# Fused local/global attention and Mish MLP on one core: sums of squares on ScalarE, clears on VectorE, and a new order for the first stretch

## The chip, the cores and the metric

The kernel runs on one core of one Trainium2 chip. The metric is the device time of one execution in microseconds (us). Lower is better. TensorE (PE) does the matmuls, VectorE (DVE), ScalarE (ACT) and GpSimd (POOL) the rest of the arithmetic; SyncE (SP), ACT and POOL also issue DMA transfers, each into a queue of its own.

## What is computed

The reference, cut to what matters (8 batches, 8 heads, 512 local and 32 global rows, head size 64):

```python
s_g = scale * np.matmul(q_g, k_all.transpose(0, 1, 3, 2))
out_g = np.matmul(sm(s_g), v_all)
...
mask = np.abs(pos[:, None] - pos[None, :]) <= window
s_ll = np.where(mask, s_ll, -1000000000.0)
...
a_l = sm(s_l)
out_l = np.matmul(a_l, np.concatenate([v_g, v_l], axis=2))
...
h = x @ w_in
sp = np.where(h > 20.0, h, np.log1p(np.exp(np.minimum(h, 20.0))))
g = h * np.tanh(sp)
return (g @ w_out).astype(np.float32)
```

Attention of 512 local rows (a window of 32 and the 32 global columns) and of 32 global rows, then a two-layer MLP of width 2048 over all 4352 rows. The two weight matrices come as 64-bit floats.

## The kernel before, in words

**Precision.** Large products are made of fp16 pieces: each operand is scaled by a power of two and split into a high and a low half (three matmuls in place of one). So each tensor needs a scale before it can be split: for a weight matrix from the sum of squares of its entries (bf16 matmuls, `ws`, line 646, and `w_norm`), for a batch's values V from their largest magnitude: `b_max` (line 717) runs five `tensor_reduce` on DVE (lines 729 and 733) into the columns of `vmx`, takes their maximum (line 735), POOL reduces it over the partitions (line 740), and `b_scale` makes the scale `sv` from it. The scale need not be the largest magnitude; anything that bounds the values within the range of fp16 does.

**Weights.** Each matrix is loaded in 16 pieces of 512 KB of raw 64-bit words (`w_load`, lines 598 and 601; the first five issued by ACT, the rest by POOL). DVE turns the words into 32-bit floats in three instructions a piece (`w_bits` line 616, `w_sum` lines 623 and 625). The raw words of the first 16 pieces use seven places in turn, so piece k + 7 can only be loaded when DVE has finished piece k. Then come the norm, the scale `sw`, and the splits (lines 694 to 700).

**The first stretch.** The program begins with loads (`ORDER` and the loop behind it): `qk` tiles of 704 KB (one per head pair of batch 0: queries and keys), `consts` of 272 KB (the mask and an identity matrix), `vraw` of 1024 KB and `vgraw` of 64 KB (batch 0's values), and the weights. For each head pair and tile of 128 rows PE makes scores `s` (line 880), DVE adds the mask and takes the row's extreme in one instruction (`row_max`, line 906, which reads `consts`), ACT takes the exponential (line 915), the probabilities are turned (in batch 0's first half by PE, lines 956 and 970) and multiplied by V (`U`, line 1005), DVE normalizes (`x`, line 1015), PE turns `x` (`XT`, lines 981 and 989), and from the x of all four head pairs the MLP's first matmuls run (`h`, line 1158). In names such as `s_1_0`, the last head pair and half come in this order.

**What sets the order.** Tasks are given to a planner (`Plan`), which lays them on the engines by costs; `moved` then applies a table `MOVES`: "91 P 271" takes task 91 out of its lane and puts it on PE's lane behind task 271 (-1: at the front). Each engine then executes its lane strictly in that order. `kept` (line 428) makes tiles that have to be cleared once: three `P`, two `ph`, four `vc`, four `vgg`, one `gph`, by memsets on POOL. A `partition_all_reduce` on a tile `warm` (line 1862) runs once on POOL ahead of the others. DMA issues of SP and ACT use eight semaphores in turn; an issue waits until the transfer that used its semaphore last has landed.

Of the kernel before, what the change touches and what calls it, by code (L numbers as in the profile page):

```python
# [71 lines left out]

MOVES = [(int(n), e, int(m)) for n, e, m in (x.split() for x in """91 P 271, 92 P 91, 93 P 92, 307 P 95, 284 P 275, 154 P 313, 350 P 154, 318 P 159, 164 P 330, 169 P 422, 174 P 343, 175 P 348, 358 P 356, 176 P 358, 447 P 376, 177 P 378, 178 P 392,
389 P 397, 415 P 461, 179 P 421, 180 P 453, 454 P 180, 181 P 454, 450 P 474, 182 P 450, 183 P 510, 184 P 183, 468 P 184, 533 P 185, 532 P 516, 513 P 556, 565 P 526, 573 P 565, 580
P 562, 625 P 629, 35 V 18, 36 V 19, 37 V 20, 38 V 22, 232 V 39, 233 V 46, 43 V 233, 47 V 43, 44 V 47, 261 V 50, 262 V 54, 58 V 262, 56 V 62, 282 V 67, 283 V 71, 291 V 283, 296 V
291, 76 V 296, 267 V 81, 72 V 267, 73 V 83, 78 V 87, 292 V 88, 115 V 292, 111 V 115, 112 V 268, 274 V 297, 107 V 327, 101 V 107, 108 V 309, 103 V 322, 298 V 103, 104 V 298, 113 V
104, 116 V 380, 328 V 116, 352 V 329, 127 V 366, 131 V 127, 373 V 424, 129 V 133, 374 V 129, 381 V 136, 407 V 139, 137 V 407, 387 V 137, 403 V 387, 388 V 144, 370 V 388, 151 V 370,
371 V 151, 413 V 371, 372 V 413, 414 V 372, 418 V 414, 408 V 418, 384 V 408, 385 V 145, 148 V 448, 383 V 153, 431 V 156, 412 V 161, 419 V 158, 449 V 419, 471 V 449, 149 V 471, 420
V 149, 466 V 420, 396 V 466, 434 V 166, 446 V 459, 163 V 171, 168 V 172, 173 V 168, 429 V 173, 472 V 429, 186 V 529, 511 V 480, 473 V 511, 534 V 188, 483 V 189, 457 V 483, 191 V
410, 478 V 522, 512 V 478, 540 V 524, 535 V 540, 489 V 535, 444 V 195, 906 V 444, 530 V 906, 500 V 530, 220 V 536, 907 V 220, 550 V 571, 552 V 260, 520 V 560, 583 V 520, 584 V 583,  # L80
587 V 585, 590 V 587, 280 V 649, 569 V 280, 639 V 569, 620 V 639, 961 V 960, 554 V 961, 786 V 554, 962 V 610, 1001 V 643, 644 V 1001, 575 V 1003, 687 V 1004, 657 V 1005, 621 V
1035, 1208 V 658, 678 V 1036, 667 V 678, 1037 V 631, 1209 V 632, 637 V 683, 1039 V 724, 813 V 1039, 779 V 734, 761 V 790, 744 V 816, 1127 V 744, 1146 V 1127, 826 V 817, 1147 V 826,
787 V 823, 834 V 787, 797 V 834, 1148 V 797, 798 V 876, 802 V 798, 837 V 802, 235 A 226, 294 A 286, 295 A 294, 105 A 304, 317 A 105, 316 A 314, 312 A 316, 325 A 312, 326 A 335, 355
A 340, 342 A 438, 345 A 342, 440 A 344, 402 A 440, 349 A 357, 359 A 349, 364 A 362, 416 A 377, 417 A 382, 451 A 417, 430 A 451, 395 A 445, 433 A 395, 427 A 458, 452 A 427, 469 A
452, 479 A 469, 428 A 479, 456 A 476, 190 A 482, 192 A 443, 538 A 192, 539 A 538, 514 A 194, 544 A 527, 229 A 548, 528 A 229, 570 A 528, 549 A 570, 519 A 259, 551 A 519, 909 A 563,
567 A 582, 568 A 567, 646 A 626, 656 A 627""".split(","))]
# [1857 lines left out]
```

## Time and profile before

| | before |
|---|---|
| median of 3 runs | 875.17 us (873.54 to 877.06) |
| the profiled execution: its own time | 874.79 us |
| its span in the trace | 873.0 us |
| PE busy | 841.1 us (96%) |
| DVE busy | 747.4 us (86%) |
| ACT busy | 645.9 us (74%) |
| POOL busy | 169.8 us (19%) |
| DMA moved | 111.07 MB |

Busy time is the time in which an engine executes instructions; DMA issues and waits are not in it. The profiled execution took 1.8 us longer than its span, and 0.4 us less than the median of the runs. All stretches below are in microseconds from the span's start.

### The profile page before, as it was taken

What the parts mean: (1) busy time and instruction counts of PE and PEld (TensorE: products, weight loads), DVE (VectorE), ACT (ScalarE), POOL (GpSimd) and SP (SyncE); (2) the same over time, 40 slices, a digit from 0 to 9 for tenths busy, and PEclk for the clock granted to TensorE, in tenths of its full rate; (3) what the DMA queues carried; (4) which work ended last, traced back from release to release, by engine and by line L of the source; (5) the groups of instructions that cost most, each with busy time, mean ns of one, the idle gap of its engine ahead of it and who ended that gap; (6) DMA issues with size and microseconds to landing.
All of it is one profiled execution on the core that took longest, in us unless ns stands there. A gap on an engine that the chain in (4) does not pass through costs nothing.

```text
span 873.0 us, 24744 instructions
## 1 busy us (share of the span) xinstructions
PE 841.1 (96%) x9792; PEld 621.1 (71%) x9792; DVE 747.4 (86%) x1989; ACT 645.9 (74%) x1389; POOL 169.8 (19%) x324
## 2 busy tenths in 40 slices
PE   2789999999999999999999999999999999999997
...
DVE  6998999758897799999879986998789999986675
...
DMA  9978566365998976769566785475757641000000
GB/s 366 372 251 182 125 153 122 58 142 105 183 205 133 191 131 136 145 111 188 125 119 101 171 135 99 91 161 121 121 120 118 89 77 38 1 26 14 14 26 26
DMA packets 206886, 111.07 MB, mean 127 GB/s; under 512 B 186993, under 2 KB 191281, under 8 KB 205745
## 3 DMA queue, kind: packets, MB, share of 16 engines
...
q14 instruction: 41, 0.33, 0.1%
...
## 4 chain that ended last, share of the span: by engine, by line
PE 89%; DVE 6%; DMA 3%; ACT 1%; issue 0%; POOL 0%; DVEq 0%; ACTq 0%; POOLq 0%
PE o L1422 33%; PE h L1327 25%; PE h L1158 12%; PE s L880 5%; PE U L1005 5%; PE o L1517 5%; DMA W<-in_w 2%; PE g L1043 1%; PE gu L1109 1%; DVE W L623 1%; DVE W L625 1%; DMA pt<-ph 1%; DVE W L616 1%; PE hx L1517 1%; PE ws L646 1%; DVE P L906 1%
## 5 line engine op out<-in xcount | busy, mean ns | idle before, releaser
L1422 PE MATMUL o<-W,G 128*128 128x512 f16 x1344 | 313.4, 379 | 0.0
L1422 PEld LDWEIGHTS <-G 128*128 128x128 f16 x1344 | 124.8, 98 | 128.7 <-issue 3.0
L1327 PEld LDWEIGHTS <-W 128*128 128x128 f16 x2880 | 166.0, 98 | 9.6 <-issue 0.2
L915 ACT ACTIVATE P<-P,nm 128x192 f32<-128x192 f32 (+1 forms) x256 | 117.8, 461 | 36.9 <-DVE nm L906 36.2
L1158 PE MATMUL h<-xh,W 128*128 128x256 f16 x640 | 114.4, 273 | 0.0
L1158 PEld LDWEIGHTS <-W 128*128 128x128 f16 x960 | 91.1, 98 | 16.8 <-issue 3.3
L1327 PE MATMUL h<-xh,W 128*128 128x128 f16 x1056 | 97.0, 219 | 0.0
L1327 PE MATMUL h<-xl,W 128*128 128x128 f16 x528 | 91.1, 219 | 0.0
L1158 PE MATMUL h<-xl,W 128*128 128x256 f16 x320 | 87.2, 272 | 0.0
L1327 PE MATMUL h<-raw,W 128*128 128x128 f16 x1152 | 73.2, 219 | 0.0
L839 POOL DMA_DIRECT2D vc<-vf x81 | 41.0, 509 | 155.9 <-DVE vf L820 110.8
L1005 PEld LDWEIGHTS <-pt 128*128 128x128 f16 (+1 forms) x1424 | 56.2, 98 | 18.1 <-issue 7.5
L880 PE MATMUL s<-qk 64*128 64x224 f16 (+3 forms) x640 | 56.4, 301 | 7.6 <-DMA qk<-in_qk 6.7
L527 ACT ACTIVATE ph<-P 128x384 f16<-128x384 f32 (+1 forms) x112 | 58.7, 538 | 4.3 <-DMA pt<-ph 3.2
L906 DVE CUSTOM_DVE_ANT_0 P<-s,consts,sq 128x192 f32<-128x192 f32 (+1 forms) x128 | 52.8, 427 | 10.4 <-PE s L880 10.4
L839 POOL DMA_DIRECT2D vgg<-vgf x84 | 44.3, 532 | 84.3 <-issue 42.3
L1005 PE MATMUL U<-vc,pt 96*128 96x64 f16 (+1 forms) x656 | 52.3, 193 | 0.0
L906 DVE CUSTOM_DVE_ANT_0 P<-s,consts 128x192 f32<-128x192 f32 (+1 forms) x128 | 45.2, 366 | 7.5 <-PE s L880 3.9
L1005 PE MATMUL U<-vf,pt 128*128 128x64 f16 x720 | 50.7, 194 | 0.1
L915 ACT ACTIVATION_READ_ACCUMULATOR P<-P,nm 128x1 f32 x256 | 48.1, 188 | 0.0
L520 ACT COPY EE<-h 128x512 f32<-128x512 f32 x47 | 27.2, 578 | 23.7 <-PE h L1327 16.6
L934 DVE SCALAR_TENSOR_TENSOR ph<-P,ph 128x256 f16<-128x256 f32 x112 | 38.3, 351 | 4.2 <-ACT ph L527 3.6
...
## 6 DMA issues: line engine op xcount, KB each, us to landing
qk<-in_qk SPq DMA_DIRECT2D x32, 704.0 KB, 5.1
W<-in_w POOLq DMA_DIRECT2D x17, 512.0 KB, 7.1
...
vraw<-in_vm SPq DMA_DIRECT2D x8, 1024.0 KB, 5.8
raw<-in_w POOLq DMA_DIRECT2D x10, 512.0 KB, 7.2
W<-in_w ACTq DMA_DIRECT2D x5, 512.0 KB, 10.9
pt<-ph SPq DMA_TRANSPOSE x120, 3.7
vgg<-vgf POOLq DMA_DIRECT2D x84, 8.0 KB, 2.7
```

The lines of the kernel that those rows point to most:

```text
L520: A.copy(dst, src)
L527: A.activation(out=dst, in_=src, func=AF.Copy, scale=c)
L839: stream(POOL, dma(kib), lambda: G.dma_start(dst(), src()), 512, r=[r], w=[w], new=new, table="dma")
L880: T.matmul(X[s[h]][:, cols(u)], part(b, hp, i)[r, u * 128:(u + 1) * 128], part(b, hp, j)[r, KO + OWN[u]:KO + OWN[u] + WIDTH[u]], start=n = ...
L906: pl.add(DVE, (134 if b >= QF else 77) + 1.03 * w, lambda: V.tensor_tensor_reduce(out=half(P, h, w), in0=X[s][:, cols(t)], in1=mask[:, m0: ...
L915: pl.add(ACT, 460, lambda: A.activation(out=half(P, h, w), in_=half(P, h, w), func=AF.Exp, bias=X[nm], scale=-1.0, accum_out=X[sums][:, t, ...
L934: pl.add(DVE, dve(2 * (z - a)), lambda a=a, z=z, q=q, o=o: V.scalar_tensor_tensor(X[ph][:, q, :, a + o:z + o], p_src(X[P], t)[:, :, a:z], ...
L1005: T.matmul(X[u][:, t, h, :], X[pt][:k, p * 4 + (c * 2 + h if turned(b, t) else h * 2 + c), :], X[vx][:k, t, vl, h * 64:(h + 1) * 64], star ...
L1158: T.matmul(X[h][:, f * TB:(f + 1) * TB], wh(i, wl)[:, off:off + 128], X[x][:, d, o:o + TB], start=(n == 0), stop=(n == 11))
L1327: T.matmul(X[h][:, c:c + 128], form(J + jj, wl)[:, off:off + 128], x(l, d), start=(p in (1, 2, 5) and c == 0 and n == 0), stop=(n == 5), s ...
L1422: T.matmul(X[o], gp(g, blk, i)[:, f, t * 128:(t + 1) * 128], wh(8 + i, wl)[:, f * 512:(f + 1) * 512], start=(turn == 0 and n == 0), stop=( ...
L1517: T.matmul(X[o][:, cols], a_form(a, jj, f), b_form(w, jj, f), start=(fresh and n == 0), stop=(n == 11), skip_group_check=True)
```

## The change

Five parts, all in the first stretch or ahead of it.

- Batch 0's five `tensor_reduce` on DVE become five `activation` with `Square` and `accum_out` on ACT (line 722, the other branch of `b_max`), with their unused output in PSUM; the scale is then made from the largest sum of squares by one more DVE instruction. Line 735's maximum over the columns is line 726 in this branch.
- The clears of `vc`, `vgg` and `gph` go from POOL to DVE.
- The `warm` reduction is given to the planner as a reader of `consts`; the table puts it at the front of POOL's lane. The instruction itself reads `pmax` only.
- `MOVES` is another table, and it can now move tasks on POOL's and SP's lanes too ("G" and "S").
- One of its entries is "1 S 11": task 1, the load of `consts`, behind task 11, the load of the fourth `qk` tile.

```diff
-VMAX = 99
+VSQ = (0,)
...
-MOVES = [(int(n), e, int(m)) for n, e, m in (x.split() for x in """91 P 271, 92 P 91, 93 P 92, 307 P 95, 284 P 275, 154 P 313, 350 P 154, 318 P 159, 164 P 330, 169 P 422, 174 P 343, 175 P 348, 358 P 356, 176 P 358, 447 P 376, 177 P 378, 178 P 392,
...
+A 733, 836 A 833, 12 G -1, 507 G 497, 1 S 11, 244 S 213, 253 S 248, 338 S 253, 435 S 460, 436 S 435,
...
-        names = {"P": PE, "V": DVE, "A": ACT}
+        names = {"P": PE, "V": DVE, "A": ACT, "G": POOL, "S": DMA}
...
         for x in tiles:
-            G.memset(part(x), 0.0)
+            (V if tag in ("vc", "vgg", "gph") else G).memset(part(x), 0.0)
...
-        if b >= VMAX:
+        if b in VSQ:
             src = lambda: X["vraw", b][:, hp].rearrange("p a c -> p (a c)") if hp < HP else X["vgraw", b]
             n = 512 if hp < HP else 128
             pl.add(ACT, act(n) + 90, lambda: A.activation(out=junk[:, :n] if b > 1 else X["vj", b][:, :n], in_=src(), func=AF.Square, accum_out=X[m][:, hp:hp + 1]),
...
-            if b >= VMAX:
+            if b in VSQ:
                 V.tensor_scalar(q, q, TINY * TINY, None, ALU.max)
                 V.tensor_scalar(q.bitcast(I32), q.bitcast(I32), 1, 0x7F800000, ALU.logical_shift_right, ALU.bitwise_and)
                 V.tensor_scalar(q, q, 2.0 ** 63, None, ALU.mult)
...
     V.memset(pmax, 0.0)
-    pl.add(POOL, 600, lambda: G.partition_all_reduce(warm, pmax, 128, RED.max))
     for i, x in enumerate(ORDER.split()):
...
     pl.slot = None
+    pl.add(POOL, 600, lambda: G.partition_all_reduce(warm, pmax, 128, RED.max), r=["consts"])
```

The lists below are the order of the built instructions, with the semaphores that each waits for (`DMAHW0` to `DMAHW7` are the eight of the SP and ACT transfers). In those of the change the line numbers are ten higher than in the profile before.

SP's lane, its first DMA issues, before:

```order
L516 DMA qk_104<-in_qk 128x1408
L516 DMA consts<-in_consts 128x544
L516 DMA vraw_123<-in_vm 128x2048
L516 DMA vgraw_145<-in_vg 128x128
L516 DMA qk_105<-in_qk 128x1408 [waits DMAHW0_49]
L516 DMA qk_106<-in_qk 128x1408 [waits DMAHW2_49]
L516 DMA qk_107<-in_qk 128x1408 [waits DMAHW3_49]
```

and in the change (`qk_104` to `qk_107` are the four head pairs):

```order
L526 DMA qk_104<-in_qk 128x1408
L526 DMA vraw_123<-in_vm 128x2048
L526 DMA vgraw_140<-in_vg 128x128
L526 DMA qk_105<-in_qk 128x1408
L526 DMA qk_106<-in_qk 128x1408 [waits DMAHW1_49]
L526 DMA qk_107<-in_qk 128x1408 [waits DMAHW2_49]
L526 DMA consts<-in_consts 128x544 [waits DMAHW3_49]
```

The load of `consts` went from the second place to the seventh. Here semaphore 1 belongs to the first weight piece, 2 to `vraw` and 3 to the second weight piece, before `consts` takes it.

DVE's lane from the end of the clears on, before:

```order
L1861 MEMSET pmax 128x1
L616 TENSOR_SCALAR W<-W 128x2x256 [waits DMAHW1_49]
L623 SCALAR_TENSOR_TENSOR W<-W 128x2x256 [waits DVE_49]
L625 SCALAR_TENSOR_TENSOR W<-W 128x2x256 [waits DVE_49]
L1875 TENSOR_SCALAR minus<-consts 128x128 [waits DMAHW2_49]
L616 TENSOR_SCALAR W<-W 128x2x256 [waits DMAHW3_49]
L906 ISA P_76,nm_0_0_0_169<-s_0_0_0_152,consts 128x192 [waits PE_49,Pool_49]
```

and in the change:

```order
L443 MEMSET gph_102 128x640
L1871 MEMSET pmax 128x1
L626 TENSOR_SCALAR W<-W 128x2x256 [waits DMAHW1_49]
L633 SCALAR_TENSOR_TENSOR W<-W 128x2x256 [waits DVE_49]
L635 SCALAR_TENSOR_TENSOR W<-W 128x2x256 [waits DVE_49]
L916 ISA P_76,nm_0_0_0_159<-s_0_0_0_149,consts 128x192 [waits DMAHW3_49,PE_49,Pool_49]
L916 ISA nm_0_0_0_159 128x1
L626 TENSOR_SCALAR W<-W 128x2x256
```

Nine memsets now stand ahead; the first `row_max` stands directly behind weight piece 0 and waits for semaphore 3, and piece 1 stands behind it.

ACT's lane in the change (the loads `L608` are weight pieces 0 to 4):

```order
L608 DMA W<-in_w 128x1024 [waits DMAHW0_49]
L1886 ACTIVATE small<-consts 128x128 [waits DMAHW3_49]
L925 ACTIVATE P_76,sums_0_0_162<-P_76,nm_0_0_0_159 128x192 [waits DVE_49]
L925 ACTIVATE P_76,sums_0_0_162<-P_76,nm_0_0_1_165 128x192 [waits DVE_49]
L732 ACTIVATE vj_173,vmx_172<-vraw_123 128x512 [waits DMAHW2_49]
L925 ACTIVATE P_77,sums_0_0_162<-P_77,nm_0_1_1_182 128x224 [waits DVE_49,Pool_49]
L732 ACTIVATE vj_173,vmx_172<-vraw_123 128x512 [waits Activation_49] x3
L732 ACTIVATE vj_173,vmx_172<-vgraw_140 128x128 [waits DMAHW5_49,Activation_49]
```

The five squares (`L732`) stand behind `small`, which reads `consts`; before, the four exponentials stood there alone.

## Rows read from the trace of the kernel before

**Rows 1.** The page: busy tenths of PE, DVE and DMA in 40 slices of 21.8 us.

```profile
PE   2789999999999999999999999999999999999997
...
DVE  6998999758897799999879986998789999986675
...
DMA  9978566365998976769566785475757641000000
```

**Rows 2.** Busy time by stretch: us, PE, PEld, DVE, ACT, POOL; clock, DMA share, GB/s.

```profile
0.00:9.99 9.99, 2.37 (x12) 1.49 (x12) 3.16 (x6) 1.59 (x2) 9.30 (x19) 1.00 0.84 313
9.99:70.11 60.12, 42.43 (x329) 27.14 (x329) 57.16 (x167) 37.83 (x110) 15.41 (x27) 0.94 0.95 325
70.11:873.00 802.89, 796.27 (x9451) 592.47 (x9451) 687.10 (x1818) 606.51 (x1277) 145.12 (x279) 1.00 0.56 110
```

**Rows 3.** What DVE waited for between 0 and 100 us: total, times, longest.

```profile
DVE W L616 <- DMA W<-in_w: 7.3, 2, 6.0
DVE W L616 <- DMA raw<-in_w: 1.6, 1, 1.6
...
DVE rs L1013 <- ACT P L915: 0.8, 1, 0.8
DVE p L749 <- POOL p L740: 0.3, 1, 0.3
```

**Rows 4.** Timelines of DVE and PE at the stretch's ends: start, duration, instruction.

```profile
8.38 0.69 DVE L625 SCALAR_TENSOR_TENSOR W<-W 128x512 int32<-128x512 int32 x1
...
9.99 0.34 DVE L906 CUSTOM_DVE_ANT_0 P<-s,consts 128x192 f32<-128x192 f32 x1
...
69.78 0.42 DVE L1015 TENSOR_TENSOR x<-U,rs 128x256 f32<-128x256 f32 x1
...
70.34 0.41 PE L981 MATMUL XT<-consts,x 128*128 128x128 f32 x2 [1.60 <-DVE x L1015]
```

**Rows 5.** SP's issues: the timeline's rows, then the four qk issues' durations, first and last start.

```profile
1.19 0.42 SPq L516 DMA_DIRECT2D consts<-in_consts  x1
1.66 0.43 SPq L516 DMA_DIRECT2D vraw<-in_vm  x1
...
L516 SPq DMA_DIRECT2D qk<-in_qk x4: 328/366/433, 0.7 to 9.0; - x4
```

**Rows 6.** DMA issues by short windows: size, us from issue to landing.

```profile
qk<-in_qk SPq DMA_DIRECT2D x1, 704.0 KB, 5.9
W<-in_w ACTq DMA_DIRECT2D x1, 512.0 KB, 6.0
...
consts<-in_consts SPq DMA_DIRECT2D x1, 272.0 KB, 7.4
...
vraw<-in_vm SPq DMA_DIRECT2D x1, 1024.0 KB, 10.7
...
qk<-in_qk SPq DMA_DIRECT2D x1, 704.0 KB, 14.9
```

**Rows 7.** Busy time and DMA from 3 to 24 us, columns as in rows 2.

```profile
3.00:24.00 21.00, 7.81 (x36) 4.70 (x37) 15.96 (x46) 5.66 (x16) 12.45 (x19) 1.00 1.02 413
```

**Rows 8.** The chain of waits, 13 to 17 us: start, step, what.

```profile
13.41 0.59 DVE vmx L729
13.99 0.33 DVE W L616
14.33 1.78 DVE vmx L729 x3
...
16.44 0.19 DVE vmx L733
16.64 1.20 DVE W L623 x2
```

**Rows 9.** ACT's and POOL's timelines: the operations nearest to those added and moved.

```profile
20.72 1.93 ACT L527 ACTIVATE vf<-vraw,sv 128x512 f16<-128x512 f32 x3
...
3.73 3.61 POOL L433 MEMSET vc<- 128x1024 f16 x4
7.28 1.34 POOL L433 MEMSET vgg<- 128x256 f16 x4
8.56 1.16 POOL L433 MEMSET gph<- 128x1280 f16 x1
...
10.16 1.79 POOL L598 DMA_DIRECT2D W<-in_w  x3
...
18.00 1.32 POOL L740 PARTITION_ALL_REDUCE p<-vmx  x1 [5.35 <-DVE vmx L735]
```

More of the change, by code (lines that the diff above doesn't have):

```diff
@@ L66 @@
 STAT = 2
-VMAX = 99
+VSQ = (0,)
 PE, DVE, ACT, POOL, DMA = "PE", "DVE", "ACT", "POOL", "DMA"
-MOVES = [(int(n), e, int(m)) for n, e, m in (x.split() for x in """91 P 271, 92 P 91, 93 P 92, 307 P 95, 284 P 275, 154 P 313, 350 P 154, 318 P 159, 164 P 330, 169 P 422, 174 P 343, 175 P 348, 358 P 356, 176 P 358, 447 P 376, 177 P 378, 178 P 392,
-389 P 397, 415 P 461, 179 P 421, 180 P 453, 454 P 180, 181 P 454, 450 P 474, 182 P 450, 183 P 510, 184 P 183, 468 P 184, 533 P 185, 532 P 516, 513 P 556, 565 P 526, 573 P 565, 580
@@ L75 @@
-P 562, 625 P 629, 35 V 18, 36 V 19, 37 V 20, 38 V 22, 232 V 39, 233 V 46, 43 V 233, 47 V 43, 44 V 47, 261 V 50, 262 V 54, 58 V 262, 56 V 62, 282 V 67, 283 V 71, 291 V 283, 296 V
-291, 76 V 296, 267 V 81, 72 V 267, 73 V 83, 78 V 87, 292 V 88, 115 V 292, 111 V 115, 112 V 268, 274 V 297, 107 V 327, 101 V 107, 108 V 309, 103 V 322, 298 V 103, 104 V 298, 113 V
-104, 116 V 380, 328 V 116, 352 V 329, 127 V 366, 131 V 127, 373 V 424, 129 V 133, 374 V 129, 381 V 136, 407 V 139, 137 V 407, 387 V 137, 403 V 387, 388 V 144, 370 V 388, 151 V 370,
@@ L81 @@
-587 V 585, 590 V 587, 280 V 649, 569 V 280, 639 V 569, 620 V 639, 961 V 960, 554 V 961, 786 V 554, 962 V 610, 1001 V 643, 644 V 1001, 575 V 1003, 687 V 1004, 657 V 1005, 621 V
-1035, 1208 V 658, 678 V 1036, 667 V 678, 1037 V 631, 1209 V 632, 637 V 683, 1039 V 724, 813 V 1039, 779 V 734, 761 V 790, 744 V 816, 1127 V 744, 1146 V 1127, 826 V 817, 1147 V 826,
-787 V 823, 834 V 787, 797 V 834, 1148 V 797, 798 V 876, 802 V 798, 837 V 802, 235 A 226, 294 A 286, 295 A 294, 105 A 304, 317 A 105, 316 A 314, 312 A 316, 325 A 312, 326 A 335, 355
@@ L84 @@
-A 340, 342 A 438, 345 A 342, 440 A 344, 402 A 440, 349 A 357, 359 A 349, 364 A 362, 416 A 377, 417 A 382, 451 A 417, 430 A 451, 395 A 445, 433 A 395, 427 A 458, 452 A 427, 469 A
-452, 479 A 469, 428 A 479, 456 A 476, 190 A 482, 192 A 443, 538 A 192, 539 A 538, 514 A 194, 544 A 527, 229 A 548, 528 A 229, 570 A 528, 549 A 570, 519 A 259, 551 A 519, 909 A 563,
-567 A 582, 568 A 567, 646 A 626, 656 A 627""".split(","))]
+MOVES = [(int(n), e, int(m)) for n, e, m in (x.split() for x in """231 P 74, 84 P 79, 225 P 211, 91 P 237, 281 P 239, 92 P 281, 251 P 92, 269 P 251, 93 P 269, 271 P 94, 234 P 271, 307 P 99, 287 P 273, 289 P 275, 284 P 289, 293 P 299, 303 P 301,
@@ new lines @@
+305 P 310, 350 P 313, 320 P 318, 422 P 386, 353 P 348, 174 P 356, 175 P 174, 358 P 175, 447 P 376, 176 P 378, 177 P 176, 178 P 392, 461 P 415, 179 P 421, 180 P 453, 454 P 180, 181
+P 454, 182 P 474, 510 P 182, 183 P 475, 450 P 183, 184 P 450, 468 P 184, 185 P 468, 533 P 185, 513 P 537, 526 P 558, 577 P 565, 573 P 577, 559 P 595, 664 P 642, 562 P 664, 580 P
+562, 665 P 580, 680 P 665, 681 P 680, 574 P 681, 622 P 574, 703 P 622, 704 P 703, 625 P 629, 645 P 625, 666 P 645, 669 P 673, 745 P 669, 705 P 745, 747 P 684, 715 P 690, 716 P 691,
@@ new lines @@
+751 P 725, 746 P 751, 748 P 731, 818 P 783, 197 V 28, 198 V 29, 221 V 30, 13 V 32, 35 V 33, 36 V 35, 20 V 36, 37 V 34, 22 V 37, 38 V 22, 25 V 38, 23 V 25, 39 V 23, 40 V 42, 241 V
+40, 232 V 43, 233 V 46, 261 V 50, 54 V 51, 266 V 55, 59 V 58, 62 V 262, 282 V 63, 267 V 282, 283 V 67, 291 V 68, 296 V 291, 76 V 296, 73 V 86, 87 V 73, 292 V 83, 88 V 292, 111 V
+268, 327 V 111, 112 V 107, 274 V 112, 115 V 108, 109 V 101, 308 V 109, 297 V 328, 309 V 297, 119 V 322, 104 V 298, 116 V 104, 117 V 113, 323 V 117, 120 V 323, 380 V 120, 123 V 351,
@@ new lines @@
+405 V 123, 124 V 365, 366 V 124, 125 V 366, 423 V 125, 131 V 128, 424 V 131, 425 V 129, 135 V 132, 439 V 133, 373 V 439, 136 V 373, 374 V 136, 406 V 374, 441 V 406, 370 V 140, 387
+V 370, 384 V 387, 407 V 384, 388 V 407, 381 V 388, 143 V 381, 371 V 137, 413 V 141, 372 V 413, 414 V 372, 151 V 414, 152 V 144, 385 V 145, 153 V 385, 448 V 153, 408 V 448, 383 V
+148, 431 V 156, 418 V 431, 412 V 157, 419 V 412, 158 V 419, 149 V 158, 420 V 149, 449 V 420, 466 V 449, 396 V 466, 166 V 396, 459 V 166, 401 V 161, 446 V 401, 434 V 446, 467 V 162,
@@ new lines @@
+171 V 467, 163 V 171, 172 V 163, 429 V 167, 472 V 173, 465 V 472, 473 V 186, 480 V 473, 511 V 480, 534 V 188, 189 V 534, 457 V 189, 483 V 457, 529 V 512, 478 V 529, 524 V 522, 540
+V 193, 444 V 540, 530 V 195, 525 V 530, 489 V 525, 531 V 489, 500 V 531, 906 V 500, 907 V 220, 545 V 907, 908 V 545, 230 V 908, 571 V 542, 583 V 550, 260 V 583, 520 V 560, 278 V
+561, 584 V 278, 910 V 578, 585 V 958, 590 V 587, 620 V 590, 648 V 591, 959 V 648, 280 V 959, 649 V 280, 960 V 649, 961 V 569, 554 V 961, 639 V 554, 786 V 639, 599 V 623, 962 V 624,
@@ new lines @@
+610 V 962, 1001 V 643, 1002 V 644, 1003 V 1002, 575 V 1003, 1004 V 575, 1005 V 687, 1035 V 657, 621 V 658, 1208 V 621, 688 V 1208, 1036 V 678, 1209 V 1036, 650 V 667, 631 V 650,
+1037 V 631, 632 V 1037, 661 V 632, 784 V 661, 636 V 682, 810 V 683, 785 V 810, 637 V 785, 696 V 637, 721 V 697, 811 V 721, 812 V 706, 689 V 812, 654 V 707, 655 V 723, 1039 V 655,
+813 V 1039, 675 V 813, 700 V 675, 676 V 724, 1062 V 676, 815 V 737, 763 V 772, 729 V 763, 1063 V 729, 850 V 1063, 730 V 850, 1064 V 730, 752 V 693, 753 V 718, 1066 V 767, 1123 V
@@ new lines @@
+768, 776 V 1123, 1124 V 821, 805 V 1124, 1125 V 822, 734 V 774, 735 V 779, 761 V 790, 744 V 816, 1127 V 744, 1146 V 1127, 826 V 817, 1147 V 826, 823 V 1147, 787 V 823, 834 V 787,
+797 V 834, 1148 V 797, 798 V 876, 802 V 798, 837 V 802, 15 A 200, 223 A 210, 243 A 238, 240 A 243, 250 A 240, 264 A 270, 286 A 294, 252 A 286, 288 A 295, 290 A 276, 311 A 300, 302
+A 311, 304 A 302, 326 A 316, 312 A 326, 354 A 319, 355 A 340, 342 A 438, 345 A 342, 440 A 345, 402 A 344, 325 A 402, 349 A 357, 391 A 362, 364 A 391, 416 A 377, 417 A 382, 451 A
@@ new lines @@
+417, 430 A 451, 394 A 411, 399 A 394, 395 A 399, 445 A 433, 400 A 445, 427 A 400, 428 A 427, 452 A 428, 469 A 464, 463 A 469, 470 A 479, 455 A 470, 462 A 455, 476 A 462, 456 A 476,
+521 A 456, 477 A 521, 482 A 477, 443 A 190, 518 A 443, 192 A 518, 538 A 192, 488 A 538, 539 A 488, 194 A 539, 219 A 499, 527 A 219, 544 A 527, 229 A 541, 570 A 548, 519 A 549, 909
+A 259, 551 A 909, 279 A 564, 586 A 279, 567 A 638, 568 A 567, 711 A 609, 627 A 647, 677 A 656, 713 A 677, 630 A 713, 635 A 630, 1038 A 670, 671 A 686, 653 A 720, 674 A 653, 699 A
```

5 lines of the change are left out of this document (2 added, 3 removed).

## Prediction

> **What bounds the kernel now.** I read the page first, then busy time by stretch, then the waits and timelines of the first 70 us, then each load's time to landing. The page shows PE nearly full from the fourth slice on and not before [rows 1]: whatever the change does can only count in the first 70 us or so, unless it adds PE work, and it adds none. By stretch this is sharper [rows 2]: from 70.11 us on PE works 796.27 of 802.89 us, so that part has a fixed length and merely starts earlier or later. Up to 70.11 us PE works 2.37 + 42.43 = 44.8 us and stands for 25.3 us.
>
> What sets the 70.11 us? At 69.78 us DVE makes the last of head pair 3's `x` and the turn of it on PE, which all MLP matmuls of the first block need, starts as soon as it is there (PE had waited 1.60 us for it) [rows 4]. And DVE is busy 57.16 of the 60.12 us between its first `row_max` (9.99) and the end of that instruction (70.11) [rows 2]. Its waits are few: 6.0 us for the first weights, later 1.3 us for weights, 0.8 us for ACT, 0.3 us for POOL [rows 3]. So the first stretch is DVE's lane, executed in order: **start of the first `row_max` plus 57.2 us of DVE work plus some 3 us of gaps**, and the end of the kernel follows it one for one.
>
> **The change, part by part.**
>
> *The loads of SP: `consts` is seventh instead of second.* This is the term that decides. In the trace SP's loads land in the order of issue: `qk` issued at 0.73 lands 5.9 us later at 6.6; `consts`, only 272 KB and issued at 1.19, lands 7.4 us later at 8.6, behind it; `vraw`, issued at 1.66, lands 10.7 us later at 12.4; the fourth `qk`, issued at 9.0, lands 14.9 us later at 23.9 [rows 5, 6]. Meanwhile the DMA is full: 413 GB/s from 3 to 24 us at a busy share of 1.02 [rows 7]. So a load's landing is given by the bytes ahead of it, not by its own size. By 23.9 us all of SP's first seven loads are in (4176 KB), in whatever order they stood. With `consts` last of them it is `consts` that lands at about that time. Beside them the weights go: five pieces by ACT, and by POOL three (pieces 5 to 7). Piece 8 needs the place of piece 1, which stands behind the `row_max` in DVE's new lane. That makes 4176 + 8 x 512 = 8272 KB or 8.47 MB: 3.13 MB by 9.99 us (313 GB/s [rows 2]), the other 5.34 MB at 413 GB/s in 12.9 us, so the last byte moves at 22.9 us and lands somewhat later. From both readings I take **23.7 us**. The low bound is 21.0 us, if two of the eight pieces (1.05 MB, 2.5 us) end later than `consts`; the high bound 25.5 us, if one more piece's time and half a microsecond of landing go in.
>
> In the new order DVE does weight piece 0 (to 9.0 us, as now [rows 4]) and then waits for `consts` with the first `row_max`. Behind that wait stand weight pieces 1 to 31, every other `row_max` and everything that follows. ACT stands too: `small` waits for `consts`, and all five squares stand behind `small`. PE has nothing but the scores of head pair 0 and piece 0's norm. So the first `row_max` moves from 9.99 to 23.7: **+13.7 us**, and nothing else can use DVE's 14.7 idle us.
>
> *Squares on ACT.* From DVE go four reductions (0.59 + 1.78 = 2.37 us) and the small one (0.19) [rows 8]: -2.6 us. DVE gets one more tiny instruction for the scale, about 0.2 us by the small one's row. ACT gets four of 128x512; the nearest row is the scaling of the same `vraw` tiles, 1.93 us for three [rows 9], so 0.64 us each, 2.9 us with the small one. ACT works 37.83 of the 60.12 us [rows 2], so the work fits. But the squares now hang on the wait above and lie between `row_max` and the scale. Counting from `consts`: `small` 0.3, two exponentials (waiting for DVE) to about 1.5, a square to 2.2, an exponential to 3.4, three squares and the small one to 5.9; DVE arrives at the maximum after 4.9 us of its lane. It waits about 1.1 us, and then 0.3 us for POOL's reduction (1.32 us [rows 9], with two weight instructions, 1.2 us, beside it [rows 8]). Bounds: 0.5 us, if ACT's steps overlap better; 4 us, if the exponentials and squares go strictly one behind the other and DVE's first steps are slow.
>
> *Other DVE work that changes sides.* The scaled identity and one of the four high halves of V come from ACT to DVE: 0.2 and 0.33 us, the latter by a weight instruction of the same 128x512 [rows 8]. `minus` and piece 1's first instruction now come behind the first `row_max` instead of ahead of it (+0.15 and +0.33). At the last `x` the new lane has done one weight instruction fewer (-0.33). In sum with the squares: -2.6 + 0.2 + 0.2 + 0.33 + 0.15 + 0.33 - 0.33 = **-1.7 us** of DVE work between the two marks; bounds -2.6 (the additions free) and -0.5.
>
> *Clears on DVE.* POOL needs 3.61 + 1.34 + 1.16 = 6.1 us for them [rows 9]. No row has a large memset of DVE. At POOL's price DVE, free from 0.8 us, ends at 6.9, when piece 0 lands (0.77 + 6.0 = 6.8 [rows 6]); at nothing it ends at 0.8. Either way it costs 0 to 0.1 us, and the wait for `consts` covers even that. It lets POOL begin its weight loads some 3 to 5 us earlier than 10.16 [rows 9]; the DMA is full by then, so this brings no byte sooner. It only moves pieces 5 and 6 ahead of parts of `vraw` and the `qk` tiles.
>
> *The rest of the order* moves PE and ACT work within the stretch. The PE lane ahead of the turn of the last `x` has the same work but for one group of four `ws` matmuls, so I cost it at nothing; PE has 17 idle us in the stretch to cover it [rows 2].
>
> **Sum.** First `row_max` at 23.7; work 57.2 - 1.7 = 55.5; gaps 1.4 for ACT and POOL and the 0.6 us of issue gaps that today's stretch has (60.12 - 57.16 = 2.96, less the three waits of 2.4 that I replace): 57.5 us. The last `x` is ready at 81.2 instead of 70.11: **+11.1 us**. On the profiled execution's 874.8 us this is 885.9; the median of the runs shown is 0.4 us above that execution. I forecast **886 us**. Break-even lies where `consts` lands at 70.1 - 57.5 = 12.6 us.
>
> **The rivals.** About 0.5% (4.4 us) is what a measurement of this kernel can tell from no change.
>
> 1. *The load does not wait behind the `qk` tiles* (not slower). If SP's small last load overtook the three large ones, it would land as soon as it is issued plus a latency. SP can't issue it before `vraw` is in: the fourth `qk` stands ahead and waits for that semaphore. `vraw` lands at 12.4 today; `consts` has gone from ahead of it (-0.7 us) and POOL's pieces come in beside, so again about 12. With 2 us for issue and landing (today it trails the `qk` tile ahead of it by 2.0 us) the first `row_max` is at about 14, the end +1.4 us: 876. It decides below 17.0 us (12.6 + 4.4). Against it: `consts` landed 2 us after the `qk` tile ahead of it, and the fourth `qk` 15 us after its issue [rows 5, 6]. The Trainium skill (DMA: Bandwidth & Descriptors, section on queues, rings and completion order) says that completion is not first in, first out per issuing engine, a later transfer may finish ahead of an earlier one; taken that far it gives this rival's 876. In this trace no load of SP did. Chance 0.09.
> 2. *The late start breaks more than it shifts.* The lane was ordered for loads that come in as they do now. If after the wait the value copies of batch 0, the refilled weights (piece 8 is issued only after 26 us) or ACT become the limit, DVE waits again. One such wait the size of the largest that DVE has today for weights while loads run (1.6 us [rows 3]) on each of two to five occasions gives 889 to 894. For it: all pieces from 8 on start some 14 us later. Against it: at 413 GB/s a piece takes the DMA 1.3 us, and DVE's three instructions for it take 1.5 us (0.33 and two of 0.60 [rows 8]) beside much else, so the loads catch up. Chance 0.09.
> 3. *The stall is covered.* If DVE's lane were not the limit, the 2.6 us taken from it and the removed gaps would show: 870 to 872. It would need a mask in place by 8.6 as today. The built order excludes this. Chance 0.02.
>
> **How the numbers follow.** The forecast has 0.80. Its own range: landing 21.0 to 25.5 (-2.7, +1.8), waits 0.5 to 4 (-0.9, +2.6), work -2.6 to -0.5 (-0.9, +1.2); not all at once: 882 to 890. Reaching some way to the rivals, 880 to 891 holds eight in ten and a little more. Slower by over 0.5% (above 879.5): forecast, second rival and a part of the first, 0.90; within 0.5%: 0.08; faster by more: 0.02.
>
> **What would show it.** Right: DVE's largest wait early on is the first `row_max` for `consts`, 12 to 16 us; `consts` takes over 10 us from issue to landing and lands after the fourth `qk`; the last `x` of head pair 3 comes near 81 us, and PE's idle time grows by 11 us, all of it before that. ACT's squares come after the wait, at 0.6 to 0.7 us each. Wrong: `consts` landing before 17 us, or DVE's work between the marks 5 us longer or shorter than 55.5.

## The result, and the profile after

The changed kernel takes **886.46 us** (median of 4, 885.76 to 887.05), the kernel before 876.01 us on the same chip: a ratio of 1.0115, 95% interval 1.0086 to 1.0144. Timed once more at the end of the study it took 886.65 us against 875.4 us, 1.0127 (1.0103 to 1.0150). One execution of experiment 2's kernel took 2235.26 us, stands alone and is left out of that kernel's figures. The profiled execution took 886.92 us with a span of 885.1 us, 12.1 us more than before. Line numbers of the changed kernel are higher by 10 behind the table and the new branches.

The page of the changed kernel, busy tenths of PE, DVE and DMA in 40 slices of 22.1 us:

```profile
PE   1679999999999999999999999999999999999997
...
DVE  2899999867797799899979987899879989997675
...
DMA  9589457364698975778565765476766541000000
```

Against [rows 1] PE and DVE differ by more than a tenth in the first slice alone: DVE falls there from 6 to 2, while the DMA is as full as it was (in the second slice it falls from 9 to 5). Busy time by stretch, cut at the first `row_max` and the end of the last `x` of head pair 3 (us, PE, PEld, DVE, ACT, POOL; granted clock, DMA share, GB/s):

```profile
0.00:24.05 24.05, 2.37 (x12) 1.49 (x12) 4.92 (x14) 1.44 (x2) 5.29 (x13) 1.00 0.90 352
24.05:81.33 57.28, 42.88 (x325) 26.83 (x325) 55.34 (x166) 39.55 (x118) 13.25 (x24) 0.91 0.76 251
81.33:885.10 803.77, 796.57 (x9456) 592.77 (x9455) 687.34 (x1818) 607.26 (x1278) 144.42 (x279) 1.00 0.55 110
```

Beside [rows 2] this is the whole account: the first `row_max` starts 14.06 us later, the stretch is 2.84 us shorter (57.28 for 60.12), and the rest 0.88 us longer (803.77 for 802.89). The sum is +12.1 us.

The 0.88 us of the rest do not come with the change. When the same kernel was profiled again at the end of the study, the first `row_max` started at 24.13, the stretch was 57.29 and the rest 802.58 us, a span of 884.0. Of the thirteen traces of this study, the five in which DVE does not wait for a `raw` load (a later weight load) behind the last `x` have a rest of 802.58 to 802.67 us, the eight in which it waits 1.2 to 2.7 us for one 802.89 to 805.10. What decides over that wait is not shown. The change itself thus costs some 11 to 12 us of span.

What DVE waited for between 0 and 100 us (total, times, longest), to be read against [rows 3]:

```profile
DVE P L916 <- DMA consts<-in_consts: 15.7, 1, 15.7
DVE W L626 <- DMA W<-in_w: 2.2, 1, 2.2
DVE W L626 <- DMA raw<-in_w: 1.3, 1, 1.3
DVE vmx L736 <- ACT vj L732: 1.1, 1, 1.1
...
DVE xh L532 <- PE XT L991: 0.4, 1, 0.4
```

One wait holds everything. DVE's timeline shows where it stands and what surrounds it, PE's the turn of the last `x`, to be read against [rows 4]:

```profile
0.90 2.11 DVE L443 MEMSET vc<- 128x512 uint32 x4 [0.90 <-PEq L1943]
2.99 0.59 DVE L443 MEMSET vgg<- 128x128 uint32 x4
3.65 0.59 DVE L443 MEMSET gph<- 128x640 uint32 x1
...
7.69 0.69 DVE L635 SCALAR_TENSOR_TENSOR W<-W 128x512 int32<-128x512 int32 x1
24.05 0.36 DVE L916 CUSTOM_DVE_ANT_0 P<-s,consts 128x192 f32<-128x192 f32 x1 [15.67 <-DMA consts<-in_consts]
...
30.11 0.16 DVE L736 TENSOR_REDUCE vmx<-vmx 128x1 f32<-128x5 f32 x1 [1.12 <-ACT vj L732]
...
81.00 0.42 DVE L1025 TENSOR_TENSOR x<-U,rs 128x256 f32<-128x256 f32 x1
```

```profile
81.57 0.41 PE L991 MATMUL XT<-consts,x 128*128 128x128 f32 x2
```

Weight piece 0 is done at 8.4 us, and the next thing DVE does is at 24.05. The reason is on SP. Its timeline, then landings by short windows of issue (size, us to landing); compare [rows 5, 6]:

```profile
0.73 0.41 SPq L526 DMA_DIRECT2D qk<-in_qk  x1
1.19 0.42 SPq L526 DMA_DIRECT2D vraw<-in_vm  x1
1.65 0.43 SPq L526 DMA_DIRECT2D vgraw<-in_vg  x1
2.13 8.79 SPq L526 DMA_DIRECT2D qk<-in_qk  x3
10.96 0.43 SPq L526 DMA_DIRECT2D consts<-in_consts  x1
```

```profile
vraw<-in_vm SPq DMA_DIRECT2D x1, 1024.0 KB, 9.4
...
qk<-in_qk SPq DMA_DIRECT2D x1, 704.0 KB, 15.5
...
qk<-in_qk SPq DMA_DIRECT2D x1, 704.0 KB, 12.6
...
consts<-in_consts SPq DMA_DIRECT2D x1, 272.0 KB, 12.9
```

`consts` is issued at 10.96 us, 9.8 us later than before, and needs 12.9 us more, though it is the smallest but one of SP's loads: it lands at 23.9 us, just behind the fourth `qk` (issued at 10.59, in at 23.2). ACT's timeline shows the squares behind it, and ACT itself waiting for `consts`:

```profile
23.89 0.31 ACT L1886 ACTIVATE small<-consts 128x128 f16<-128x128 f32 x1 [21.88 <-DMA consts<-in_consts]
...
28.17 0.60 ACT L732 ACTIVATE vj<-vraw 128x512 f32<-128x512 f32 x1
28.70 0.19 ACT L732 ACTIVATION_READ_ACCUMULATOR vj<-vraw 128x1 f32 x1
```

### The profile page after: what moved, and what is told of

It reads as the page before. It is cut to its first block, busy times and chain, and to the rows that moved or that the text cites. A ratio compares the mean times of both kernels' runs of the same rounds, so it can differ in the third digit from the quotient of the medians.

```text
span 885.1 us, 24749 instructions
## 1 busy us (share of the span) xinstructions
PE 841.8 (95%) x9792; PEld 621.1 (70%) x9792; DVE 747.6 (84%) x1996; ACT 648.3 (73%) x1397; POOL 163.0 (18%) x315
## 4 chain that ended last, share of the span: by engine, by line
PE 86%; DVE 5%; issue 4%; DMA 3%; ACT 1%; POOL 1%; SPq 0%; DVEq 0%; POOLq 0%; ACTq 0%
PE o L1432 33%; PE h L1337 25%; PE h L1168 10%; PE s L890 5%; PE U L1015 5%; PE o L1527 4%; DMA consts<-in_consts 1%; PE g L1053 1%; PE gu L1119 1%; DMA vraw<-in_vm 1%; DMA raw<-in_w 1%; DVE W L635 1%; DVE W L633 1%; PE hx L1527 1%; DVE W L626 0%
## 5 line engine op out<-in xcount | busy, mean ns | idle before, releaser
L1168 PEld LDWEIGHTS <-W 128*128 128x128 f16 x960 | 91.1, 98 | 16.9 <-issue 3.0
L916 DVE CUSTOM_DVE_ANT_0 P<-s,consts 128x192 f32<-128x192 f32 (+1 forms) x128 | 45.7, 369 | 24.1 <-DMA consts<-in_consts 15.7
L530 ACT COPY EE<-h 128x512 f32<-128x512 f32 x47 | 27.2, 579 | 23.7 <-PE h L1337 16.7
L947 DVE SCALAR_TENSOR_TENSOR ph<-P,ph 128x448 f16<-128x448 f32 x64 | 39.4, 617 | 2.9 <-ACT ph L537 2.2
## 6 DMA issues: line engine op xcount, KB each, us to landing
W<-in_w ACTq DMA_DIRECT2D x5, 512.0 KB, 11.9
```

What stands on the lines that cost most here:

```text
L530: A.copy(dst, src)
L916: pl.add(DVE, (134 if b >= QF else 77) + 1.03 * w, lambda: V.tensor_tensor_reduce(out=half(P, h, w), in0=X[s][:, cols(t)], in1=mask[:, m0: ...
L947: pl.add(DVE, dve(n), lambda: V.scalar_tensor_tensor(p_part(X[ph], t, 1), p_src(X[P], t), PSC, p_part(X[ph], t, 0), ALU.mult, ALU.subtract ...
L1168: T.matmul(X[h][:, f * TB:(f + 1) * TB], wh(i, wl)[:, off:off + 128], X[x][:, d, o:o + TB], start=(n == 0), stop=(n == 11))
```

## The experiments

The theory from the traces: the place of `consts` on SP's queue is the loss, nearly all of it, and the other parts of the change save a little. All times below are medians beside runs of the kernel before on the same chip (874.59 us for experiments 1 to 4, 874.76 for 5, 7 and the first run of 9, 874.82 for 6 and 8, 875.4 for the second run of 9 and the change beside it); the spans are those of single profiled executions.

**1. The constants second again**, all else as changed.

```diff
-12 G -1, 507 G 497, 1 S 11, 244 S 213,
+12 G -1, 507 G 497, 244 S 213,
```

> The change with the one entry that moves the load of consts taken out of the table: consts is SP's second load again, all else (squares on ACT, clears on DVE, the new lanes) stays. Theory A (the late consts costs everything, and the rest of the change is a small gain on DVE's lane): consts lands near 8.6 us, the first row_max starts near 9 us, the last x of head pair 3 is ready near 66 to 67 us (57.3 us later, as in the changed kernel), the time is 871 to 873 us. Rival B (the new lanes or the squares cost the time): consts lands early, but the time stays at 883 to 886 us.

Measured: 875.62 us, ratio 1.0010 (1.0001 to 1.0019), span 874.1. One entry of the table accounts for 11.0 of the 12.1 us of span. But the other half of the expectation missed: without its late load the change should have been faster than the kernel before by some 3 us, and it is not faster at all. The waits of DVE up to 100 us say why:

```profile
DVE W L626 <- DMA W<-in_w: 7.5, 4, 2.7
DVE W L626 <- DMA raw<-in_w: 1.5, 1, 1.5
```

and its timeline, the pieces behind the first `row_max` (8.85 us):

```profile
13.95 0.43 DVE L626 TENSOR_SCALAR W<-W 128x512 int32<-128x512 int32 x1 [2.29 <-DMA W<-in_w]
...
16.71 0.43 DVE L626 TENSOR_SCALAR W<-W 128x512 int32<-128x512 int32 x1 [1.60 <-DMA W<-in_w]
...
21.00 0.43 DVE L626 TENSOR_SCALAR W<-W 128x512 int32<-128x512 int32 x1 [0.93 <-DMA W<-in_w]
```

DVE waits 2.29 + 1.60 + 0.93 = 4.8 us for weights behind the mark, where the kernel before, after its first weights, waits 7.3 - 6.0 = 1.3 us for a piece and 1.6 us for `raw` in all of 100 us [rows 3]. Experiments 5 and 6 follow this up.

**2. The kernel before with the constants seventh**, nothing else of the change. (The two added letters let the table move loads; no other entry uses them.)

```diff
-567 A 582, 568 A 567, 646 A 626, 656 A 627""".split(","))]
+567 A 582, 568 A 567, 646 A 626, 656 A 627, 2 S 12""".split(","))]
-        names = {"P": PE, "V": DVE, "A": ACT}
+        names = {"P": PE, "V": DVE, "A": ACT, "G": POOL, "S": DMA}
```

> The kernel before with its consts load moved behind the fourth qk load and nothing else. Theory A: consts lands near 24 us, DVE stands at its first instruction that reads it (minus, now at 8.99 us), the last x is ready near 84 us, some 14 us late, the time is 888 to 890 us, worse than the change, since the 1.7 us that the change takes off DVE's lane are missing. Rival B: 875 to 877 us.

Measured: 891.21 us (median of three), ratio 1.0189 (1.0174 to 1.0204), span 890.2, a little above the expectation. The load's place by itself costs 17.2 us of span, more than the whole change does. DVE waits 14.7 us for `consts`, and its stretch from the first `row_max` is 61.34 us, 4.06 us longer than the changed kernel's. So with `consts` late the other parts of the change do save: 890.2 - 885.1 = 5.1 us, of which 4.06 us lie in the stretch. The squares are 1.2 to 1.5 us of these (experiment 9); how the remainder divides between the new order and the clears, no run tells.

**3 and 4. The constants fifth or fourth on SP**: behind the second `qk`, or behind `vgraw`.

```diff
-1 S 11,
+1 S 7,
```

```diff
-1 S 11,
+1 S 4,
```

> The change with consts behind the second qk load (fifth of SP's loads instead of seventh). Theory A with SP's loads landing in order of issue: consts lands 1 to 1.5 us after the second qk, which landed at 17.7 us in the change, so near 19 us; the last x near 76 us; the time 881 us, 5 us below the change. If order did not matter and only the wait for a semaphore held the load back, it would land near 13 to 14 us and the time would be 876 us.

> The change with consts behind the values' loads (fourth of SP's loads). Theory A: vgraw landed at 13.4 us in the change, so consts lands near 14 us, the last x is ready near 71.5 us, the time is 876 to 877 us: about what the kernel before takes, although the load lands some 5.5 us later than there. Rival B: 883 to 886 us.

Measured: 883.8 us, 1.0106 (1.0093 to 1.0119), span 881.1; and 879.63 us, 1.0056 (1.0044 to 1.0068), span 877.1. Both are some 3 us above what was expected. The prediction's formula gives them once the start is known: 20.71 + 57.5 + 802.89 and the 1.8 us around the span are 882.9, with 16.91 it is 879.1, and the profiled executions took 882.88 and 878.94. So what the expectation missed was mainly when the constants land: 20.5 us where it had near 19, and 16.7 us where it had near 14. (Experiment 3's profiled execution is also the fastest of its four.) With the two ends, by busy time in stretches cut at the first `row_max` and the end of the last `x`:

| `consts` on SP's queue | first `row_max` | stretch | rest | span |
|---|---|---|---|---|
| second | 8.85 | 61.38 | 803.87 | 874.1 |
| fourth | 16.91 | 57.52 | 802.67 | 877.1 |
| fifth | 20.71 | 57.78 | 802.61 | 881.1 |
| seventh (the change) | 24.05 | 57.28 | 803.77 | 885.1 |

From the fourth place on a microsecond of delay is a microsecond of time: the first `row_max` is 7.14 us later, the last `x` 6.90, and the span 8.0 us longer, 1.1 of it in the rest. From the second to the fourth it is not: 8.06 us later, the last `x` 4.20 us later, the span 3.0 us longer. The difference is in the stretch, 3.86 us: the 4.8 us of waits for weights, less the 1.1 us wait for the squares, which only the later places have. What DVE loses to `consts` there it would lose to weights otherwise.

**5. The constants second, and the clears back on POOL.**

```diff
-12 G -1, 507 G 497, 1 S 11, 244 S 213,
+12 G -1, 507 G 497, 244 S 213,
-            (V if tag in ("vc", "vgg", "gph") else G).memset(part(x), 0.0)
+            G.memset(part(x), 0.0)
```

> The constants' load is second again and the three groups are cleared by GpSimd as before; the squares and the compute orders stay as changed. Reading: with the constants second the other parts of the change brought nothing (875.6 us, where 871 to 873 had been expected) because VectorE then waits three times for weight pieces, 2.3, 1.6 and 0.9 us, and these land late because GpSimd, freed of the clears, starts its first two pieces of 512 KB at 4.6 us rather than 10.2. Theory A (those two pieces take the bandwidth): GpSimd's loads start near 10 us again, the fourth weight piece of ScalarE's queue lands near 14 us rather than 16.6, the fifth near 18 rather than 21, VectorE's waits for weights behind the first row maximum fall from 4.8 us to 2 or less, last x of head pair 3 near 67 us, 871 to 873 us. Rival B (the pieces are late for another reason, such as the order on ScalarE's own queue): no change, 875 to 876 us.

Measured: 873.06 us, ratio 0.9983 (0.9972 to 0.9995), span 872.3. POOL issues its first weights at 10.09 us rather than 4.59. ACT's fourth weight load lands 11.7 us after its issue instead of 14.5, the fifth 11.1 instead of 14.1. In experiment 1 (POOL's first weight issue, then ACT's fourth and fifth weight load: size, us from issue to landing):

```profile
4.59 1.28 POOL L608 DMA_DIRECT2D W<-in_w  x2
...
W<-in_w ACTq DMA_DIRECT2D x1, 512.0 KB, 14.5
...
W<-in_w ACTq DMA_DIRECT2D x1, 512.0 KB, 14.1
```

and here:

```profile
10.09 1.79 POOL L608 DMA_DIRECT2D W<-in_w  x3
...
W<-in_w ACTq DMA_DIRECT2D x1, 512.0 KB, 11.7
...
W<-in_w ACTq DMA_DIRECT2D x1, 512.0 KB, 11.1
```

The last `x` ends at 67.20 us instead of 70.23, at the place that theory A named. Of those 3.0 us the span keeps 1.8: the rest is 805.10 us, 1.2 us longer than in experiment 1. There PE's work behind the mark is 0.34 us more and its idle time 0.9 us more: PE waits 0.5 us for a DMA into `pt` and 0.4 us for DVE's `nm`, two waits that experiment 1's trace has not. This profiled execution is 1.0 us above the median of its twelve.

**6. The constants second, the clears on DVE, and POOL's loads held until the constants are in.** POOL's warming reduction reads a column of them, and its loads stand behind it.

```diff
-12 G -1, 507 G 497, 1 S 11, 244 S 213,
+12 G -1, 507 G 497, 244 S 213,
-    pl.add(POOL, 600, lambda: G.partition_all_reduce(warm, pmax, 128, RED.max), r=["consts"])
+    pl.add(POOL, 600, lambda: G.partition_all_reduce(warm, ident[:, 0:1], 128, RED.max), r=["consts"])
```

> The constants' load is second, VectorE clears as the change has it, and GpSimd's warming reduction takes its input from the constants, so that its weight loads start when these have landed, near 9 us, not at 4.6. It parts the two things that the run with the clears on GpSimd had together. Theory A (the start of GpSimd's loads is all that counts, not the clears): the fourth weight piece near 14 us, VectorE's waits for weights behind the first row maximum 2.5 us or less, last x of head pair 3 at 66.5 to 68 us, 872 to 873.5 us, as with the clears on GpSimd. Rival B (the clears themselves matter): 875 us or more, or below 871 us should the first weight operation gain from an idle GpSimd (1.30 us beside the clears, 0.43 us without).

Measured: **872.6 us, ratio 0.9976 (0.9967 to 0.9984)**: of all kernels of this study the lowest ratio. It is a quarter of a percent below the kernel before, and its interval lies below experiment 1's; it overlaps experiment 5's, so which of these two is faster is not shown. Its profiled execution is the slowest of its twelve (874.88 us, span 873.0). DVE's timeline of it, the same three pieces as in experiment 1:

```profile
12.35 0.43 DVE L626 TENSOR_SCALAR W<-W 128x512 int32<-128x512 int32 x1 [1.02 <-DMA W<-in_w]
...
14.29 0.43 DVE L626 TENSOR_SCALAR W<-W 128x512 int32<-128x512 int32 x1 [0.78 <-DMA W<-in_w]
...
18.57 0.43 DVE L626 TENSOR_SCALAR W<-W 128x512 int32<-128x512 int32 x1 [0.34 <-DMA W<-in_w]
```

and POOL's:

```profile
8.45 0.36 POOL L1884 PARTITION_ALL_REDUCE warm<-consts  x1 [4.66 <-DMA consts<-in_consts]
8.67 1.79 POOL L608 DMA_DIRECT2D W<-in_w  x3
```

Only the start of POOL's loads moved, from 4.59 to 8.67 us, and the waits fell from 4.8 to 2.1 us (a fourth, of 0.31 us, comes later). ACT's fourth and fifth weight loads land 12.1 and 11.9 us after their issue, where experiment 1 has 14.5 and 14.1, and the last `x` ends at 68.25 instead of 70.23. So it is the loads, not the clears: two pieces of 512 KB that DVE needs only behind 20 us took the way from the three that it needed at 12 to 20.

**7. Six weight pieces ahead of the wait.** The change as it is, but what DVE could do while it waits for `consts` is put there.

```diff
+AHEAD = [(n, DVE, m) for n, m in zip((29, 30, 31, 42, 43, 44, 32, 33, 34, 46, 47, 48, 35, 36, 37, 38, 39, 40), (28, 29, 30, 31, 42, 43, 44, 32, 33, 34, 46, 47, 48, 35, 36, 37, 38, 39))] + [(53, POOL, 21)]
...
+        for n, e, m in AHEAD:
+            lanes[e].remove(n)
+            lanes[e].insert(lanes[e].index(m) + 1, n)
```

> The change as it is, the constants' load seventh, but on VectorE six weight pieces (18 instructions, some 1.65 us a piece, 10 us in all) stand ahead of the first row maximum instead of behind it; GpSimd's fourth load stays behind the reduction of the maxima, so that no transfer starts sooner. Theory A (VectorE is what sets the end and loses the stall only because it takes its instructions in order): the wait for the constants falls from 15.7 us to 8 or less in several pieces, first row maximum still at 24 us, last x of head pair 3 near 72 us, 875 to 879 us. Rival B (behind the constants the chain of scores, exponentials, squares and value copies on TensorE and ScalarE is as long as VectorE's own work): VectorE idles behind the first row maximum instead, last x at 78 us or later, 882 to 886 us.

Measured: 885.75 us, ratio 1.0122 (1.0107 to 1.0136), span 884.7. Rival B, plainly. DVE works 15.61 us ahead of the first `row_max` instead of 4.92, and 46.16 instead of 55.34 us behind it; yet the stretch shrinks by 0.86 us. Its waits up to 100 us (L numbers higher by 5):

```profile
DVE P L921 <- PE PT L971: 4.1, 1, 4.1
DVE vmx L741 <- ACT vj L737: 3.6, 1, 3.6
...
DVE xh L537 <- PE XT L996: 1.2, 1, 1.2
...
DVE P L921 <- DMA consts<-in_consts: 0.5, 1, 0.5
DVE p L760 <- POOL p L755: 0.5, 1, 0.5
DVE vgf L778 <- ACT vgf L776: 0.4, 1, 0.4
```

The wait for `consts` is gone (0.5 us) and 4.1 + 3.6 + 1.2 + 0.5 + 0.4 = 9.8 us of others stand behind it, where the change has 1.1 + 0.4: the 8.3 us more are the 9.2 us of work less the 0.86. The weights had been the cover for the squares on ACT and for PE's transposes.

**8. The values' work ahead of the wait too.** Experiment 7, and on ACT the five squares, the lows and two value copies ahead of `small`, on DVE the maximum, the scale and its part of the lows ahead of the first `row_max`.

```diff
-39))] + [(53, POOL, 21)]
+39))] + [(20, DVE, 34), (22, DVE, 37), (25, DVE, 40)] + [(n, ACT, m) for n, m in zip((15, 16, 17, 18, 19, 24, 201, 210), (9, 15, 16, 17, 18, 19, 24, 201))] + [(53, POOL, 21)]
```

> The kernel with six weight pieces ahead of the first row maximum, and beside them the values' work that needs no constants: ScalarE's five squares, the scaled lows and two scaled copies ahead of its copy of the constants, VectorE's maximum, the scale's arithmetic and its part of the lows ahead of the first row maximum. Reading of the run before: the 10 us that VectorE gained came back as waits, 3.6 us for the squares, 0.5 us for GpSimd and 4.1 us for TensorE's transposes, because ScalarE and TensorE also take their work in order and the squares stood behind the copy of the constants. Theory A (the stall costs what stands behind the constants on all three engines, so with that moved too the end comes early): those waits fall below 1 us each, last x of head pair 3 at 72 to 75 us, 877 to 881 us. GpSimd's weight loads start earlier in it and may push the constants by up to 1.3 us. Rival B (the chain from scores over exponentials and transposes is bound otherwise, by buffers or by the transfers of vc): last x at 79 us or later, 883 to 886 us.

Measured: 883.19 us, ratio 1.0096 (1.0082 to 1.0109), span 881.4: 3.3 us of span better than experiment 7. The time is within rival B's, but the last `x` starts at 76.85 us, between the marks of the two theories. DVE's waits up to 90 us:

```profile
DVE P L921 <- PE PT L971: 3.7, 1, 3.7
DVE P L921 <- DMA consts<-in_consts: 2.8, 1, 2.8
```

The waits for the squares and for POOL are gone, so these were in-order waits, as theory A had it. The one for `PT` stays. And POOL, freed earlier by the scale, loads weights from 17 us on: the first `row_max` starts at 26.77, 2.5 us later than in experiment 7 (the expectation had allowed 1.3). From there to the end of the last `x` it takes 50.42 us, 44.99 of them DVE's work: the stretch is 6.9 us shorter than the change's, and the span 3.7 us. In the `PT` wait DVE's seventh `row_max` instruction wants a buffer of `P` (the kernel has three) that PE must first transpose; on PE these transposes stand behind the turns of the values (`VT`), which need the constants. Whether a fourth buffer would end it was not tried.

**9. Batch 0's reductions back on DVE**, the rest as changed; run twice, the second time beside the change itself.

```diff
-            pl.add(ACT, act(n) + 90, lambda: A.activation(out=junk[:, :n] if b > 1 else X["vj", b][:, :n], in_=src(), func=AF.Square, accum_out=X[m][:, hp:hp + 1]),
+            pl.add([(ACT, act(n) + 90), (DVE, 1500)], 0, lambda e: V.tensor_reduce(out=X[m][:, hp:hp + 1], in_=src(), axis=AX.X, op=ALU.max, apply_absolute_value=True),
...
-            if b in VSQ:
+            if False:
...
-15 A 200,
+15 V 222, 16 V 15, 17 V 16, 18 V 17, 19 V 18,
```

> The change as it is, the constants' load seventh, but batch 0's five reductions run on VectorE again (as maxima, with the arithmetic of the kernel before behind them), right behind the fourth row maximum; every other instruction stands where the change has it. Theory A (VectorE's work behind the constants counts one for one): 2.7 us of reductions come back and the wait of 1.1 us for ScalarE's squares goes, so the end moves by 1.3 to 2.7 us: 887 to 889 us on a chip where the change takes 886. Rival B (the squares freed nothing on the path): within 0.5 us of the change, 885.5 to 886.5 us.

> The changed kernel itself, so that the runs with the constants seventh have their reference on the same chip and against the same runs of the kernel before: a ratio of 1.010 to 1.014 is expected, as when it was first timed.

> Batch 0's reductions on VectorE, once more, beside the changed kernel on one chip. Its first look had the last x of head pair 3 1.5 us later than the change and the span only 0.4 us longer. Theory A (VectorE's work behind the constants counts one for one to the end): 1 to 2.5 us longer than the change. Rival B (what the squares save is given back behind the first stretch): within 0.5 us of it.

Measured: 887.2 us, 1.0145 (1.0132 to 1.0158); then 887.53 us, 1.0139 (1.0114 to 1.0165), beside the change's 886.65 us, 1.0127 (1.0103 to 1.0150). The intervals overlap, so of the time itself only the medians speak: 0.9 us. The traces are clearer. In the first run the stretch is 58.80 us against 57.28, of it DVE's work 57.68 against 55.34, and the 1.1 us wait for squares is gone; its span of 885.5 us is only 0.4 us longer because its rest is 802.64 us against 803.77. In the second pair the rests are alike (802.64 and 802.58), the last `x` starts at 82.33 us against 81.09, and the spans are 885.3 and 884.0. So by the traces the squares are worth 1.2 to 1.5 us of the stretch, at the lower end of theory A's range; the times alone, 0.9 us apart, do not show it clear of noise.

## Why the prediction came out right, point by point

*The loads of SP* (taken: `consts` in at 23.7 us, between 21.0 and 25.5). It landed at 23.9 and the first `row_max` started at 24.05. In the change and in each place that experiments 2 to 4 gave the constants they landed behind the load issued ahead of them: at 24.0 us in experiment 2, 20.5 in 3, 16.7 in 4. The prediction's count of bytes held too: up to the first `row_max` the DMA moved 352 GB/s for 24.05 us, the 8.47 MB that it had added up. The Trainium skill (DMA: Bandwidth & Descriptors, section on queues, rings and completion order) says that completion is not first in, first out per issuing engine. The first rival took that as far as it goes; none of SP's first seven loads in these runs overtook another. The place on the queue priced the load to 0.2 us at the end of it, but not in the middle: in experiment 4 `consts` landed 3.3 us behind `vgraw`, though its 272 KB take 0.7 us at 413 GB/s. Two weight pieces of ACT's and POOL's landed in the same stretch (at 16.9 and 16.1 us), so what the other queues move meanwhile has to be counted as well.

*The stretch* (taken: 55.5 us of DVE work and 2.0 us of gaps). Measured 55.34 and 57.28 - 55.34 = 1.94 us. Within the gaps the wait for the squares was 1.12 us (taken 1.1) and that for POOL nothing (taken 0.3): its reduction took 0.72 us, under two weight instructions. The last `x` was ready at 81.33 instead of the 81.2 forecast.

*The squares.* The step had them give 2.6 us and take 0.2 for the scale and 1.4 in waits, 1.0 us net; experiment 9 finds 1.2 to 1.5 us of the stretch. ACT's took 0.58 to 0.60 us and 0.19 us each for reading out the sum.

*The clears, costed at 0 to 0.1 us.* DVE needs 3.3 us for them (POOL 6.1 [rows 9]) and then still waits 2.2 us for the first weights. So the number is right. **The reason beside it was not**: that POOL's earlier loads bring no byte sooner, only move two pieces ahead of parts of `vraw` and the `qk` tiles, and so need no price. They started 5.6 us earlier (3 to 5 forecast) and also came ahead of ACT's weight pieces, which DVE needs first. In the change the wait for `consts` hides this; with `consts` second it takes back all that the other parts save (experiments 1, 5, 6).

*The break-even at 12.6 us of landing.* The formula behind it, first `row_max` plus 57.5 us, holds from 16.91 us on (57.28 to 57.78), and nearly at 9.24 us where POOL's loads start late (57.96, experiment 5). It fails with `consts` early and POOL's loads early: at 8.85 us the stretch is 61.38. By it experiment 1's profiled execution should have taken 871.0 us, and it took 875.92. The step that failed is the one on the clears, carried to a place where nothing covers it.

*The end follows DVE's lane.* For a delay of the lane this held: 14.06 us in, 2.84 out of the stretch. As a statement of what bounds the stretch it was too strong. Experiment 7 took 9.2 us of work out of it and got 0.86 back, since DVE then waited for ACT's squares and PE's transposes. "Nothing else can use DVE's 14.7 idle us" was right of the order as built; of the two other orders tried, one got 0.4 us of span back and one 3.7.

*The sum.* On the profiled execution it gave 885.9 us, and 886.92 was measured: the first `row_max` 0.35 us later, the stretch 0.22 us shorter, and 0.88 us in the rest, which the sum put at nothing. That the median of 886.46 lies within half a microsecond of the forecast is in part luck: the kernel before took 876.01 us beside it, 0.8 us more than the median that the forecast started from, and the difference of the medians is 10.45 us, for 11.1 forecast.

*The rivals.* An overtaking load: not in any run. New waits of 1.6 us each: none over 1.3 us behind the first `row_max`. A covered stall: excluded by the 15.7 us wait.
